# Attention with a sine and cosine mixture: sines in two pieces, other places for the splits of x and u, values copied at once

## The chip, the cores and the metric

The kernel runs on one core of one Trainium2 chip. The metric is device time in microseconds (us), median of several runs. The engines are TensorE (PE in the profile; its weight loads are PEld), VectorE (DVE), ScalarE (ACT), GpSimd (POOL) and SyncE (SP), which here only issues DMAs.

## What is computed

The reference, cut to what matters (8 batches, 8 heads, 576 positions, head size 64, model size 512):

```python
scores = (q @ k.T) / sqrt(64)
scores = where(scores >= max(scores) - tau, scores, -1e9)
attn = softmax(scores)
x = (attn @ v), heads side by side           # (8, 576, 512)
theta = x @ w_theta
zr, zi = x * cos(theta), x * sin(theta)
u = x + w_tok_r @ zr + w_tok_i @ zi          # over the positions
out = u + maximum(u @ w_ch, 0)
```

The attention part is float32. The four weight matrices come in as 8-byte floats, which the kernel converts on the chip. Products of the second half ("the mixture") are made from a high and a low part of each factor, in a faster 32-bit format (F32R), as three matmuls.

## The kernel before

**Attention.** Two heads make a pair; there are 32 pairs (numbered from 0), four to a batch, and nine half units to a pair: 288 steps of the loop in `tile_attn_moe`. A half unit is 128 query rows against all 576 keys. `score` has PE make the scores into one PSUM tile, DVE evict them with the row minimum (L302) and ACT take the exponential (L312). `mask` (L321) applies the threshold on DVE. `flip` and `flip_last` transpose the weights on PE (L365, L378), ACT copies them out (tile `a`, L370 to L385). `values` (L398) multiplies by v, 20 matmuls, twice per pair (first 256 rows, then 320), and ACT copies the result to `xT` (L399). `normalize` transposes the reciprocals of the row sums, and `scale` in it multiplies xT by them on DVE (L425, L428). Scores run three steps ahead of flips (AHEAD = 3). Inputs of the next pair are loaded and split at fixed steps of a pair: q at its steps 1 and 2 (ACT L242, L243, POOL L245), k at 4 and 5 (ACT L100, POOL L109).

**Mixture.** When a batch's four pairs are done, `start` splits its four x tiles in high and low parts (`split_x`: a cast on ACT or DVE, L100 or L104, then a subtraction on POOL or DVE, L109) and appends a generator `moe(b)`, which issues its work in small portions while the next batch's attention runs. The order of its parts is written out by hand (`ORDER`): `angle` ("a": product with w_theta, evicted by ACT L487 and DVE L488, reduced to turns on DVE L494, absolute value on ACT L497), `sines` ("s", for two chunks at a time: the sine table is loaded on ACT, L502, four sines taken, L507, each multiplied by x on POOL, L508, and the exponential's table loaded again, L510), `flip` in `moe` ("f": transposes on PE L524, high part by ACT L526, low part by DVE L513), `token` ("t": the product over positions, L542, added to x by DVE L545), then `split_u` for each chunk of u and the product with w_ch (L591 evicts it). The first product of each kind takes chunks 0 to 2 first and chunk 3 last.

**What sets the order.** All four engines run their instructions in the order in which the code issues them; attention's are moved a little ahead by priority. In each step the loop issues the next scores, exponential and mask, then `catch_up`, `fill`, the flips, `catch_up`, then the step's `todo` (values, normalize, start) behind a second `fill`. `fill` first advances one of two streams of weight loads (`streams`, in turn), then draws from the mixture until the PE time due (`share`) is spent; a generator that yields None ends the turn. `defer` puts a function off until a given number of `catch_up` calls. Values and normalize of a pair's end come one step after its last flip, start two steps after it (LAG = 3). PSUM has one double tile for scores and six tiles of one bank (`ps_t`) for all else, so a late copy out of PSUM keeps PE waiting. The eighth batch's mixture runs after the last pair, alone (`finish`).

**Weights.** `convert` turns 8-byte floats into 4-byte ones in many small DVE and ACT steps, the last on PE (w_ps, L164, L165). `split_weight` casts the high part on ACT (L171) and subtracts it for the low part on DVE (L174); `load_wtok` keeps both in SBUF for nine chunks (two halves each), `load_wm` sends them through DRAM.

Of the kernel before, what the change touches and what calls it, by code (L numbers as in the profile page):

```python
# [10 lines left out]
F32 = mybir.dt.float32  # L11
# [28 lines left out]
def tile_attn_moe(  # L40
# [33 lines left out]

    ident = const.tile([P, P], F32, name="ident")
    make_identity(nc, ident)

    small = const.tile([P, 4], F32, name="small")
    tau_sb = small[:, 0 : 1]
# [86 lines left out]
            got.append((slice(c, c + n2), ps))  # L166
        return got, flat

    def split_weight(got, hi, lo):
        for r, w in got:  # L170
            nc.scalar.copy(out=hi[:, r], in_=w)  # L171
        yield
        for r, w in got:
            nc.vector.tensor_tensor(out=lo[:, r], in0=w, in1=hi[:, r].bitcast(F32), op=ALU.subtract)  # L174

    def load_wtok(c):
        got, _ = yield from convert(w_tok[c * P : (c + 1) * P, :], S)
# [2 lines left out]
    def load_wm(which, src, c):  # L180
        got, flat = yield from convert(src[c * P : (c + 1) * P, :], DM, which == 0)
        hi, lo = flat[:, 0, :DM], flat[:, 1, :DM]
        yield from split_weight(got, hi, lo)
        for i, t in enumerate((hi, lo)):
            nc.sync.dma_start(
                wm_dram[which, :, :, i, c, :].rearrange("m p e -> p m e"),
                t.bitcast(F32).rearrange("p (m e) -> p m e", e=P),
            )
# [90 lines left out]
    def score(u, j):  # L279

        pr = u.pr
        ps = ps_s.tile([P, 2, 512], F32, tag="s", name="s_ps")
        if u.i < 4:
            c = u.i * P + (0 if j == 0 else SP + 64)
            parts = [(pr.qf[:, c : c + P], j, kk, 0) for kk in pr.keys[j]]
        else:
            parts = [(pr.qf[:, 512:SP], 0, kk, 0) for kk in pr.keys[0]]
            parts += [(pr.qf[:, S : S + P], 1, kk, 64) for kk in pr.keys[1]]
        for h in range(2):
            todo = []  # L290
            for st, jj, kk, turn in parts:
                k0 = (h * HS + turn) % S
                n1 = min(HS, S - k0)
                todo.append((st, 0, n1, kk[:, k0 : k0 + n1]))
                if n1 < HS:
                    todo.append((st, n1, HS, kk[:, 0 : HS - n1]))
            for x, (st, d0, d1, kk) in enumerate(todo):
                nc.tensor.matmul(ps[:, h, d0:d1], st, kk, start=(x == 0), stop=(x == len(todo) - 1))  # L298

        sc = pool.tile([P, S], F32, tag="sc", name="sc", bufs=2)  # L300
        u.ps.append(sc)
        nc.vector.tensor_scalar(  # L302
            out=sc.rearrange("p (a b) -> p a b", a=2),
            in0=ps[:, :, :HS],
            scalar1=-1.0,
            scalar2=None,
            op0=ALU.mult,
            op1=ALU.min,
            accum_out=u.nm[:, j : j + 1],
        )  # L310

        nc.scalar.activation(out=u.s[:, j], in_=sc, func=AF.Exp, bias=u.nm[:, j : j + 1], scale=-1.0)  # L312
        if j == u.m - 1:
            nc.vector.tensor_scalar(
                out=u.nm[:, 2 : 2 + u.m], in0=u.nm[:, : u.m], scalar1=span, scalar2=None, op0=ALU.add
            )

    def mask(u, j):
# [11 lines left out]
        if u.i == 4:  # L330
            defer(lambda: nc.scalar.copy(out=u.sf[:, S:SP], in_=u.sf[:, 512:S]))
            invert(u.pr)

    waiting = []

    def defer(fn, n=1):
        waiting.append([n, fn])

    def catch_up(everything=False):
        now = []  # L340
        for w in list(waiting):
            w[0] -= 1
            if w[0] <= 0 or everything:
                waiting.remove(w)
                now.append(w[1])
        for fn in now:
            fn()
# [39 lines left out]
    def values(pr, g):  # L387

        t = pr.a[g]
        w = t.w  # L390
        if pr.n not in xT:
            xT[pr.n] = pool.tile([P, S], F32, tag="xT", name=f"xT{pr.n}", bufs=8)
        o = ps_t.tile([P, 512], F32, tag="t", name="o_ps")
        for c in range(5):
            for j in range(2):
                st = pr.v[:, 4 * j + c, :] if c < 4 else pr.v5[:, j, :]
                mv = t.a[:, c, j, :] if c < 4 else t.a5
                nc.tensor.matmul(o[64 * j : 64 * j + 64, :w], st, mv, start=(c == 0), stop=(c == 4))  # L398
        defer(lambda: nc.scalar.copy(out=xT[pr.n][:, 256 * g : 256 * g + w], in_=o[:, :w]))  # L399

    def invert(pr):
        rows = pr.rows
# [11 lines left out]
    def normalize(pr):  # L414
# [12 lines left out]
                r = slice(64 * j, 64 * j + 64)  # L427
                nc.vector.tensor_tensor(out=x[r, 512:S], in0=x[r, 512:S], in1=tl[r, 64 * j : 64 * j + 64], op=ALU.mult)  # L428

        defer(scale, 2)  # L430

    def product(wm, parts, todo, together):

# [30 lines left out]
    def split_x(b):  # L464
        parts[b] = []
        for c in range(NM):
            hi, lo = halves("x")
            split(nc.vector if c == NM - 1 else nc.scalar, nc.vector if c == NM - 1 else nc.gpsimd, hi, lo, xT[b * NP + c])
            parts[b].append((hi, lo))

    def moe(b):
        last = b == B - 1
# [7 lines left out]
        def angle(m):  # L480
# [13 lines left out]
            nc.vector.scalar_tensor_tensor(  # L494
                out=th, in0=km, scalar=MAGIC, in1=th, op0=ALU.subtract, op1=ALU.subtract
            )
            defer(lambda: nc.scalar.activation(out=km, in_=th, func=AF.Abs))  # L497
            zs[m, "f"] = z

        def sines(ms):  # L500

            nc.scalar.preload_act_table(AF.Sin)  # L502
            for m in ms:
                z = zs.pop((m, "f"))
                x = xT[b * NP + m]
                for zi, scale, bias in ((z[:, :S], -TURN_IN, half_pi), (z[:, S:], -TURN_IN, 0.0)):
                    nc.scalar.activation(out=zi, in_=zi, func=AF.Sin, scale=scale, bias=bias)  # L507
                    lo_eng.tensor_tensor(out=zi, in0=zi, in1=x, op=ALU.mult)  # L508
                zs[m] = z
            nc.scalar.preload_act_table(AF.Exp)  # L510

        def low(zl, tv, zh):
            defer(lambda: nc.vector.tensor_tensor(out=zl, in0=tv, in1=zh.bitcast(F32), op=ALU.subtract))  # L513

        def flip(m):
            z = zs.pop(m)
# [13 lines left out]
            zs[m, "T"] = out  # L530

        def token(m):
            catch_up(True)
            zz = zs.pop((m, "T"))
            x = xT[b * NP + m]
            for h in range(2):
# [4 lines left out]
                for n, (z, w) in enumerate(work):  # L541
                    nc.tensor.matmul(ps[:, :HS], z, w, start=(n == 0), stop=(n == len(work) - 1))  # L542
                    if n % 3 == 2:
                        yield 393
                nc.vector.tensor_tensor(out=x[:, hs], in0=ps[:, :HS], in1=x[:, hs], op=ALU.add)  # L545

        us = {}

        def split_u(c):
            hi, lo = halves("u")  # L550
            split(nc.vector, nc.vector if c == NM - 1 else nc.gpsimd, hi, lo, xT[b * NP + c])
            us[c] = (hi, lo)

        done = []
# [1 line left out]
        for what in ORDER.split():  # L556
# [10 lines left out]
                    yield cost  # L567
                left -= 1
            elif what == "s":
                defer(lambda ms=ms: sines(ms), 2)  # L570
                yield None
            elif what == "f":
                yield from flip(m)
            else:
# [4 lines left out]
                        yield next(other, 0)  # L579
                for cost in other:  # L580
                    yield cost
                done.append(m)
            while left == 0 and done:
                split_u(done.pop(0))
        yield None
# [20 lines left out]
    def fill():  # L606

        with at(-5, 0):
            next(streams[step[0] % 2], None)
            step[0] += 1  # L610
            if step[0] > 2 * (per + 8):
                next(late, None)
# [39 lines left out]
    with tc.manual_schedule(engines={nc.tensor.engine, nc.vector.engine, nc.scalar.engine, nc.gpsimd.engine}):  # L652
# [11 lines left out]
        for t, (n, i, j) in enumerate(halfs):  # L664
# [8 lines left out]
            with tc.high_priority(offset=ATTENTION):  # L673
                u = units[n, i]
                flip(u, j)
                if j == 1 or i == 4:
                    flip_last(u)
                    del units[n, i]
            catch_up()
            if (i, j) == (1, 1):  # L680
                todo.setdefault(t + 1, []).append((values, (pr, 0)))
            if i == 4:
                todo.setdefault(t + 1, []).extend([(values, (pr, 1)), (normalize, (pr,))])
                if n % NP == NP - 1:
                    todo.setdefault(t + LAG - 1, []).append((start, (n // NP,)))
            fill()
            with tc.high_priority(offset=ATTENTION):
                if n + 1 < B * NP:
# [17 lines left out]
        for t in sorted(todo):  # L706
            for fn, a in todo[t]:
                fn(*a)
            catch_up()
            catch_up()  # L710
        finish()


# [44 lines left out]
```

## Time and profile before

| | |
|---|---|
| median of 3 runs | 1275.32 us (1273.94 to 1278.27) |
| the profiled execution's own time | 1274.94 us |
| its span, first to last instruction | 1273.1 us |
| mean granted TensorE clock | 0.944 |
| busy: PE, DVE, ACT, POOL | 1104.8, 846.8, 756.2, 345.2 us |

An engine's busy share says little alone, as the stages differ: some 129 us of attention with weight conversion, seven stretches of about 148 to 162 us in which attention of one batch and the mixture of the batch before share PE, and a last one of some 85 us with a mixture alone. In waits, "A <- B" reads: A stood idle until B's instruction released it. The clock is the share of full speed that PE was granted (1.0 is 2.4 GHz, 0.5 is 1.2 GHz).

### The profile page before, as it was taken

The numbers are of one execution on the slowest core, as the hardware profiler recorded it, in microseconds if no ns is written. First come the engines' busy times: TensorE is split into PE (matmuls) and PEld (weight loads), VectorE is DVE, ScalarE is ACT, GpSimd is POOL, SyncE is SP. The second block draws the span as 40 slices with busy tenths as digits, with TensorE's granted clock in tenths as the row PEclk, the third lists the DMA queues.
The fourth block names the chain that finished last, engine by engine and source line by source line (L and its number), as shares of the span: only waits on it lengthen the run. The fifth ranks groups of instructions, "written<-read, shape, count | busy, mean of one in ns | idle before, by whom it ended". The sixth has DMA issues, their size and how long they took to land.

```text
span 1273.1 us, 20988 instructions
## 1 busy us (share of the span) xinstructions
PE 1104.8 (87%) x7736; PEld 961.2 (75%) x7736; DVE 846.8 (67%) x1979; ACT 756.2 (59%) x1444; POOL 345.2 (27%) x239
## 2 busy tenths in 40 slices
PE   5868786898789988899879997899888998799988
PEld 4546575787778877788768876788778887688888
DVE  6878777877557765677656765577656766567553
ACT  5656567655676556765576547765567655765350
POOL 1111143121532222421332215322224212332100
PEclk9878898999989998999989999999899999899989
DMA  6542222234211143113321142111431133210311
GB/s 216 151 120 80 62 73 75 81 114 150 79 54 47 55 125 98 44 48 97 108 78 48 48 150 79 49 50 58 125 102 40 47 89 103 91 47 1 112 59 55
DMA packets 55174, 105.24 MB, mean 83 GB/s; under 512 B 11936, under 2 KB 20128, under 8 KB 55072
## 3 DMA queue, kind: packets, MB, share of 16 engines
q1 hardware_dynamic: 55072, 103.91, 27.0%
q8 instruction: 61, 1.00, 0.3%
q14 instruction: 41, 0.34, 0.1%
HBM read 90.24 MB, written 13.63 MB: 82 GB/s over the span
## 4 chain that ended last, share of the span: by engine, by line
PE 63%; ACT 16%; DVE 13%; issue 4%; POOL 2%; DMA 0%; SPq 0%; ACTq 0%; DVEq 0%; POOLq 0%
PE y_ps L542 13%; PE o_ps L398 13%; PE m_ps L448 12%; PE s_ps L298 12%; PE t_ps L365 6%; DVE sc L302 4%; DVE s_sb L321 3%; ACT s_sb L312 2%; PE z_ps L524 2%; ACT z L507 2%; ACT L510 2%; ACT L502 2%; ACT a L370 1%; PE rb_ps L417 1%; POOL xl L109 1%
## 5 line engine op out<-in xcount | busy, mean ns | idle before, releaser
L312 ACT ACTIVATE s_sb<-sc,nm 128x576 f32<-128x576 f32 x288 | 223.7, 777 | 397.1 <-DVE sc L302 396.8
L302 DVE TENSOR_SCALAR_CACHE_REDUCE sc<-s_ps 128x576 f32<-128x576 f32 x288 | 216.8, 753 | 224.8 <-PE s_ps L298 223.1
L298 PE MATMUL s_ps<-k,qq 128*128 128x288 f32 (+1 forms) x1344 | 252.7, 315 | 57.8 <-DVE sc L302 40.7
L321 DVE SCALAR_TENSOR_TENSOR s_sb<-sc,nm,s_sb 128x576 f32<-128x576 f32 x288 | 282.0, 979 | 13.5 <-ACT s_sb L312 4.2
L298 PEld LDWEIGHTS s_ps<-k,qq 128*128 128x128 f32 x1344 | 200.3, 198 | 91.2 <-DVE sc L302 43.4
L245 POOL TENSOR_TENSOR qq<-qraw,qq 64x576 fp32r<-64x576 f32 x62 | 95.3, 1541 | 387.3 <-ACT qq L243 201.4
L542 PE MATMUL y_ps<-wt_h,zh 128*128 128x288 f32 x576 | 170.1, 313 | 24.6 <-DVE zl L513 13.1
L365 PE MATMUL t_ps<-ident,s_sb 128*128 128x128 f32 x1152 | 183.9, 285 | 0.3 <-DVE wt_l L174 0.3
L398 PE MATMUL o_ps<-a,v 128*64 128x320 f32 (+1 forms) x1280 | 172.3, 414 | 0.9 <-ACT a L370 0.9
L542 PE MATMUL y_ps<-wt_l,zh 128*128 128x288 f32 x576 | 166.3, 306 | 0.0
L109 POOL TENSOR_TENSOR k<-kraw,k 128x576 fp32r<-128x576 f32 x62 | 96.0, 1549 | 250.9 <-ACT k L100 229.7
L370 ACT COPY a<-t_ps 128x512 f32<-128x512 f32 x256 | 148.2, 579 | 24.9 <-PE t_ps L365 24.0
L365 PEld LDWEIGHTS t_ps<-ident,s_sb 128*128 128x128 f32 x1152 | 149.9, 147 | 3.2 <-issue 1.1
L398 PEld LDWEIGHTS o_ps<-a,v 128*64 128x64 f32 x1280 | 87.4, 138 | 64.3 <-issue 10.1
L542 PEld LDWEIGHTS y_ps<-wt_h,zh 128*128 128x128 f32 x576 | 111.5, 194 | 29.1 <-DVE zl L513 15.7
L448 PE MATMUL m_ps<-xh,wm 128*128 128x288 f32 x512 | 109.4, 345 | 23.6 <-ACT xh L100 23.6
L508 POOL TENSOR_TENSOR z<-z,xT 128x576 f32<-128x576 f32 x56 | 80.2, 1462 | 136.8 <-ACT z L507 136.8
L542 PEld LDWEIGHTS y_ps<-wt_l,zh 128*128 128x128 f32 x576 | 111.9, 194 | 0.0
L448 PEld LDWEIGHTS m_ps<-xh,wm 128*128 128x128 f32 x512 | 87.4, 222 | 29.3 <-ACT xh L100 29.0
L542 PE MATMUL y_ps<-wt_h,zl 128*128 128x288 f32 x576 | 102.7, 304 | 0.0
L448 PE MATMUL m_ps<-uh,wm 128*128 128x288 f32 x512 | 88.6, 310 | 0.8
L524 PE MATMUL z_ps<-ident,z 128*128 128x128 f32 x288 | 54.0, 302 | 34.9 <-ACT a L370 28.7
(81 smaller groups left out, 1534.2 us busy)
## 6 DMA issues: line engine op xcount, KB each, us to landing
wm<-wm_dram SPq DMA_DIRECT2D x64, 512.0 KB, 3.6
qraw<-in_qT_dram SPq DMA_DIRECT2D x128, 144.0 KB, 3.4
kraw<-in_kT_dram SPq DMA_DIRECT2D x128, 144.0 KB, 2.9
out_dram<-xT SPq DMA_DIRECT2D x32, 288.0 KB, 4.0
v<-in_vp_dram SPq DMA_DIRECT2D x32, 256.0 KB, 2.7
wraw<-in_w_tok_dram SPq DMA_DIRECT2D x9, 576.0 KB, 4.8
wm_dram<-wraw SPq DMA_DIRECT2D x16, 256.0 KB, 2.3
wraw<-in_w_theta_dram SPq DMA_DIRECT2D x4, 512.0 KB, 5.8
```

The lines of the kernel that those rows point to most:

```text
L109: eng_lo.tensor_tensor(out=lo, in0=src, in1=hi.bitcast(F32), op=ALU.subtract)
L245: eng.tensor_tensor(out=qq[64:128], in0=raw[64:128], in1=qq[64:128].bitcast(F32), op=ALU.subtract)
L298: nc.tensor.matmul(ps[:, h, d0:d1], st, kk, start=(x == 0), stop=(x == len(todo) - 1))
L302: nc.vector.tensor_scalar(out=sc.rearrange("p (a b) -> p a b", a=2), in0=ps[:, :, :HS], scalar1=-1.0, scalar2=None, op0=ALU.mult, op1=ALU.min,
L312: nc.scalar.activation(out=u.s[:, j], in_=sc, func=AF.Exp, bias=u.nm[:, j : j + 1], scale=-1.0)
L321: nc.vector.scalar_tensor_tensor(out=e, in0=u.ps[j], scalar=u.nm[:, 2 + j : 3 + j], in1=e, op0=ALU.is_le, op1=ALU.mult, accum_out=u.pr.row ...
L365: nc.tensor.transpose(out=tp[:, c * P : (c + 1) * P], in_=u.sf[:, k0 + c * P : k0 + (c + 1) * P], identity=ident)
L370: nc.scalar.copy(out=t.a[:, :, j, q0 : q0 + P], in_=tp.rearrange("p (c q) -> p c q", c=4))
L398: nc.tensor.matmul(o[64 * j : 64 * j + 64, :w], st, mv, start=(c == 0), stop=(c == 4))
L448: nc.tensor.matmul(tiles[h][:, :HS], wm[:, a, c, :], parts[c][bb][:, hs], start=(count[h] == 0), stop=(count[h] == 11))
L508: lo_eng.tensor_tensor(out=zi, in0=zi, in1=x, op=ALU.mult)
L542: nc.tensor.matmul(ps[:, :HS], z, w, start=(n == 0), stop=(n == len(work) - 1))
```

## The change

- A constant `minus` (the identity times -1) is made; the low parts of the token weights are made by a PE matmul that subtracts the high part in PSUM and an ACT copy, in place of a DVE subtraction.
- `split_x`: the casts of chunks 0 and 1 stay on ACT, chunk 2's goes to DVE (low part on POOL), chunk 3 (DVE, DVE) is deferred by one `catch_up`.
- `start` is issued one step earlier, in the step of the last values; `scale` is deferred by one `catch_up` in place of two; the copy of the values' result is issued at once.
- `sines` becomes a generator: one chunk a step. The first piece loads the sine table, the last loads the exponential's. An exponential that comes up between is held and issued behind the last piece. The absolute values that are still deferred are issued before a series; `token` flushes only the deferred low parts.
- Chunk 3 of u is split in halves on DVE inside `token`, behind each half's addition.
- `fill` advances only one of the two weight streams in the first seven turns (steps with an even count).
- In the tail, both sine pieces are issued on the spot.

```diff
--- before.py
+++ after.py
@@ -74,6 +74,8 @@
 
     ident = const.tile([P, P], F32, name="ident")
     make_identity(nc, ident)
+    minus = const.tile([P, P], F32R, name="minus")
+    nc.vector.tensor_scalar(out=minus, in0=ident, scalar1=-1.0, scalar2=None, op0=ALU.mult)
 
     small = const.tile([P, 4], F32, name="small")
     tau_sb = small[:, 0 : 1]
@@ -166,12 +168,16 @@
             got.append((slice(c, c + n2), ps))
         return got, flat
 
-    def split_weight(got, hi, lo):
+    def split_weight(got, hi, lo, on_pe=True):
         for r, w in got:
             nc.scalar.copy(out=hi[:, r], in_=w)
         yield
         for r, w in got:
-            nc.vector.tensor_tensor(out=lo[:, r], in0=w, in1=hi[:, r].bitcast(F32), op=ALU.subtract)
+            if on_pe:
+                nc.tensor.matmul(w, minus, hi[:, r], start=False, stop=True, skip_group_check=True)
+                nc.scalar.copy(out=lo[:, r], in_=w)
+            else:
+                nc.vector.tensor_tensor(out=lo[:, r], in0=w, in1=hi[:, r].bitcast(F32), op=ALU.subtract)
 
     def load_wtok(c):
         got, _ = yield from convert(w_tok[c * P : (c + 1) * P, :], S)
@@ -180,7 +186,7 @@
     def load_wm(which, src, c):
         got, flat = yield from convert(src[c * P : (c + 1) * P, :], DM, which == 0)
         hi, lo = flat[:, 0, :DM], flat[:, 1, :DM]
-        yield from split_weight(got, hi, lo)
+        yield from split_weight(got, hi, lo, False)
         for i, t in enumerate((hi, lo)):
             nc.sync.dma_start(
                 wm_dram[which, :, :, i, c, :].rearrange("m p e -> p m e"),
@@ -309,7 +315,13 @@
             accum_out=u.nm[:, j : j + 1],
         )
 
-        nc.scalar.activation(out=u.s[:, j], in_=sc, func=AF.Exp, bias=u.nm[:, j : j + 1], scale=-1.0)
+        def exponential():
+            nc.scalar.activation(out=u.s[:, j], in_=sc, func=AF.Exp, bias=u.nm[:, j : j + 1], scale=-1.0)
+
+        if held[0]:
+            held.append(exponential)
+        else:
+            exponential()
         if j == u.m - 1:
             nc.vector.tensor_scalar(
                 out=u.nm[:, 2 : 2 + u.m], in0=u.nm[:, : u.m], scalar1=span, scalar2=None, op0=ALU.add
@@ -331,16 +343,36 @@
             defer(lambda: nc.scalar.copy(out=u.sf[:, S:SP], in_=u.sf[:, 512:S]))
             invert(u.pr)
 
+    held = [False]
+    series = []
+
+    def sine_piece():
+
+        if not series:
+            return
+        if not held[0]:
+            nc.scalar.preload_act_table(AF.Sin)
+            held[0] = True
+        if next(series[0], None) is None:
+            series.pop(0)
+            if not series:
+                nc.scalar.preload_act_table(AF.Exp)
+                now = held[1:]
+                held[:] = [False]
+                for fn in now:
+                    fn()
+
     waiting = []
 
-    def defer(fn, n=1):
-        waiting.append([n, fn])
-
-    def catch_up(everything=False):
+    def defer(fn, n=1, kind=None):
+        waiting.append([n, fn, kind])
+
+    def catch_up(only=None):
         now = []
         for w in list(waiting):
-            w[0] -= 1
-            if w[0] <= 0 or everything:
+            if only is None:
+                w[0] -= 1
+            if w[0] <= 0 or only is not None and w[2] == only:
                 waiting.remove(w)
                 now.append(w[1])
         for fn in now:
@@ -396,7 +428,7 @@
                 st = pr.v[:, 4 * j + c, :] if c < 4 else pr.v5[:, j, :]
                 mv = t.a[:, c, j, :] if c < 4 else t.a5
                 nc.tensor.matmul(o[64 * j : 64 * j + 64, :w], st, mv, start=(c == 0), stop=(c == 4))
-        defer(lambda: nc.scalar.copy(out=xT[pr.n][:, 256 * g : 256 * g + w], in_=o[:, :w]))
+        nc.scalar.copy(out=xT[pr.n][:, 256 * g : 256 * g + w], in_=o[:, :w])
 
     def invert(pr):
         rows = pr.rows
@@ -427,7 +459,7 @@
                 r = slice(64 * j, 64 * j + 64)
                 nc.vector.tensor_tensor(out=x[r, 512:S], in0=x[r, 512:S], in1=tl[r, 64 * j : 64 * j + 64], op=ALU.mult)
 
-        defer(scale, 2)
+        defer(scale)
 
     def product(wm, parts, todo, together):
 
@@ -465,8 +497,13 @@
         parts[b] = []
         for c in range(NM):
             hi, lo = halves("x")
-            split(nc.vector if c == NM - 1 else nc.scalar, nc.vector if c == NM - 1 else nc.gpsimd, hi, lo, xT[b * NP + c])
             parts[b].append((hi, lo))
+            if c < 2:
+                split(nc.scalar, nc.gpsimd, hi, lo, xT[b * NP + c])
+            elif c == 2:
+                split(nc.vector, nc.gpsimd, hi, lo, xT[b * NP + c])
+            else:
+                defer(lambda: split(nc.vector, nc.vector, hi, lo, xT[b * NP + c]), 1)
 
     def moe(b):
         last = b == B - 1
@@ -494,23 +531,22 @@
             nc.vector.scalar_tensor_tensor(
                 out=th, in0=km, scalar=MAGIC, in1=th, op0=ALU.subtract, op1=ALU.subtract
             )
-            defer(lambda: nc.scalar.activation(out=km, in_=th, func=AF.Abs))
+            defer(lambda: nc.scalar.activation(out=km, in_=th, func=AF.Abs), 1, "abs")
             zs[m, "f"] = z
 
         def sines(ms):
 
-            nc.scalar.preload_act_table(AF.Sin)
-            for m in ms:
+            for k, m in enumerate(ms):
                 z = zs.pop((m, "f"))
                 x = xT[b * NP + m]
                 for zi, scale, bias in ((z[:, :S], -TURN_IN, half_pi), (z[:, S:], -TURN_IN, 0.0)):
                     nc.scalar.activation(out=zi, in_=zi, func=AF.Sin, scale=scale, bias=bias)
                     lo_eng.tensor_tensor(out=zi, in0=zi, in1=x, op=ALU.mult)
                 zs[m] = z
-            nc.scalar.preload_act_table(AF.Exp)
+                yield None if k == len(ms) - 1 else True
 
         def low(zl, tv, zh):
-            defer(lambda: nc.vector.tensor_tensor(out=zl, in0=tv, in1=zh.bitcast(F32), op=ALU.subtract))
+            defer(lambda: nc.vector.tensor_tensor(out=zl, in0=tv, in1=zh.bitcast(F32), op=ALU.subtract), 1, "low")
 
         def flip(m):
             z = zs.pop(m)
@@ -530,7 +566,7 @@
             zs[m, "T"] = out
 
         def token(m):
-            catch_up(True)
+            catch_up(only="low")
             zz = zs.pop((m, "T"))
             x = xT[b * NP + m]
             for h in range(2):
@@ -543,12 +579,17 @@
                     if n % 3 == 2:
                         yield 393
                 nc.vector.tensor_tensor(out=x[:, hs], in0=ps[:, :HS], in1=x[:, hs], op=ALU.add)
+                if m == NM - 1:
+                    if h == 0:
+                        us[m] = halves("u")
+                    hi, lo = us[m]
+                    split(nc.vector, nc.vector, hi[:, hs], lo[:, hs], x[:, hs])
 
         us = {}
 
         def split_u(c):
             hi, lo = halves("u")
-            split(nc.vector, nc.vector if c == NM - 1 else nc.gpsimd, hi, lo, xT[b * NP + c])
+            split(nc.vector, nc.gpsimd, hi, lo, xT[b * NP + c])
             us[c] = (hi, lo)
 
         done = []
@@ -567,8 +608,13 @@
                     yield cost
                 left -= 1
             elif what == "s":
-                defer(lambda ms=ms: sines(ms), 2)
-                yield None
+                catch_up(only="abs")
+                series.append(sines(ms))
+                if step[0] is None:
+                    while series:
+                        sine_piece()
+                else:
+                    yield None
             elif what == "f":
                 yield from flip(m)
             else:
@@ -579,7 +625,8 @@
                         yield next(other, 0)
                 for cost in other:
                     yield cost
-                done.append(m)
+                if m < NM - 1:
+                    done.append(m)
             while left == 0 and done:
                 split_u(done.pop(0))
         yield None
@@ -606,7 +653,8 @@
     def fill():
 
         with at(-5, 0):
-            next(streams[step[0] % 2], None)
+            if step[0] % 2 == 0 or step[0] > 6:
+                next(streams[step[0] % 2], None)
             step[0] += 1
             if step[0] > 2 * (per + 8):
                 next(late, None)
@@ -677,12 +725,13 @@
                     flip_last(u)
                     del units[n, i]
             catch_up()
+            sine_piece()
             if (i, j) == (1, 1):
                 todo.setdefault(t + 1, []).append((values, (pr, 0)))
             if i == 4:
                 todo.setdefault(t + 1, []).extend([(values, (pr, 1)), (normalize, (pr,))])
                 if n % NP == NP - 1:
-                    todo.setdefault(t + LAG - 1, []).append((start, (n // NP,)))
+                    todo.setdefault(t + 1, []).append((start, (n // NP,)))
             fill()
             with tc.high_priority(offset=ATTENTION):
                 if n + 1 < B * NP:
@@ -707,7 +756,8 @@
             for fn, a in todo[t]:
                 fn(*a)
             catch_up()
-            catch_up()
+        catch_up()
+        step[0] = None
         finish()
```

## Rows read from the trace of the kernel before

**Rows 1.** Page, part 1: busy time, share of the span, instructions.

```profile
PE 1104.8 (87%) x7736; PEld 961.2 (75%) x7736; DVE 846.8 (67%) x1979; ACT 756.2 (59%) x1444; POOL 345.2 (27%) x239
```

**Rows 2.** Windows: pair 13, pair 14, batch 3; us, PE, PEld, DVE, ACT, POOL busy, PEclk.

```profile
488.30:531.30 43.00, 34.10 (x236) 29.73 (x235) 23.27 (x60) 32.71 (x59) 17.41 (x12) 0.92 0.25 76
531.30:563.60 32.30, 31.45 (x244) 28.03 (x244) 23.74 (x58) 19.57 (x40) 8.95 (x6) 1.00 0.17 47
...
450.40:598.20 147.80, 131.19 (x958) 115.69 (x958) 96.96 (x232) 91.72 (x176) 45.24 (x30) 0.97 0.26 77
```

**Rows 3.** Waits of PE, batch 3 (450.4 to 598.2 us): total, times, longest.

```profile
PE z_ps L524 <- ACT a L370: 4.1, 1, 4.1
PE m_ps L448 <- ACT xh L100: 3.3, 3, 3.0
PE y_ps L542 <- DVE zl L513: 1.8, 1, 1.8
PE y_ps L542 <- ACT xT L399: 1.4, 1, 1.4
PE m_ps L448 <- DVE ul L109: 1.3, 1, 1.3
PE z_ps L524 <- DVE zl L513: 1.2, 1, 1.2
PE t_ps L378 <- ACT xT L399: 0.8, 1, 0.8
PE m_ps L448 <- POOL xl L109: 0.8, 1, 0.8
```

**Rows 4.** Timeline of ACT, 458 to 471 us: start, us, instruction, idle before.

```profile
465.30 0.78 ACT L312 ACTIVATE s_sb<-sc,nm 128x576 f32<-128x576 f32 x1 [4.78 <-DVE sc L302]
...
468.33 1.81 ACT L100 CAST xh<-xT 128x576 fp32r<-128x576 f32 x3
```

**Rows 5.** Timeline of PE, 459 to 464 us.

```profile
460.27 2.91 PE L398 MATMUL o_ps<-a,v 128*64 128x320 f32 x20
```

**Rows 6.** Timeline of DVE, 459 to 590 us.

```profile
464.44 0.76 DVE L302 TENSOR_SCALAR_CACHE_REDUCE sc<-s_ps 128x576 f32<-128x576 f32 x1 [3.61 <-PE s_ps L298]
...
585.96 1.84 DVE L109 TENSOR_TENSOR ul<-xT,uh 128x576 fp32r<-128x576 f32 x1
```

**Rows 7.** Timeline of ACT, 486 to 525 us.

```profile
489.08 0.78 ACT L312 ACTIVATE s_sb<-sc,nm 128x576 f32<-128x576 f32 x1 [1.44 <-DVE sc L302]
...
491.37 1.28 ACT L502 ACT_TABLE_LOAD   x1
...
496.56 0.62 ACT L408 COPY rb<-rows 128x512 f32<-128x512 f32 x1
...
510.15 0.78 ACT L312 ACTIVATE s_sb<-sc,nm 128x576 f32<-128x576 f32 x1 [4.46 <-DVE sc L302]
```

**Rows 8.** Windows: from the first sines, and behind them (columns as before).

```profile
491.37:505.69 14.32, 10.18 (x60) 9.60 (x60) 7.51 (x19) 12.70 (x23) 5.48 (x4) 0.76 0.17 55
498.00:504.50 6.50, 5.73 (x26) 5.73 (x27) 5.23 (x13) 4.93 (x13) 1.00 (x1) 0.50 0.01 3
```

**Rows 9.** Groups by line: busy us, mean ns, idle before.

```profile
L502 ACT ACT_TABLE_LOAD x16 | 20.5, 1283 | 0.3
...
L174 DVE TENSOR_TENSOR wt_l<-w_ps,wt_h 128x288 fp32r<-128x288 f32 x18 | 6.9, 442 | 0.0
L171 ACT CAST wt_h<-w_ps 128x288 fp32r<-128x288 f32 x18 | 6.9, 398 | 4.1 <-PE w_ps L165 4.1
```

**Rows 10.** Windows: the first batch of pairs (columns as before).

```profile
10.40:139.20 128.80, 99.72 (x541) 72.02 (x541) 106.35 (x248) 79.74 (x155) 23.72 (x16) 0.89 0.43 132
```

**Rows 11.** Waits of PE, 10.4 to 139.2 us.

```profile
PE s_ps L298 <- DVE sc L302: 24.2, 21, 3.4
```

**Rows 12.** Waits of PE, 1187 us to the end.

```profile
PE m_ps L448 <- POOL xl L109: 1.7, 2, 1.5
PE y_ps L542 <- ACT zh L526: 1.5, 1, 1.5
```

## The prediction

> **What bounds the kernel now.** I read the page's shares first, then windows, then PE's waits, then the timelines of the engines that PE waited for. TensorE (PE) is busy 87% of the span and every other engine under 70% [rows 1], so the question is where PE stands idle. The windows answer it by stage: batch 3, from the scores of its boundary to those of the next (147.8 us), holds 131.2 us of PE work, so 16.6 us idle, while its dearest pair (13 of 32, 43.0 us) alone holds 8.9 of them, with ACT busy 32.7 of 43.0 there and the clock at 0.92 [rows 2]. The waits name the places: eight waits, 14.7 us together, once each per batch (the xh one in three pieces) [rows 3]; the batches from 3 to 6 repeat them almost to the hundredth. Each belongs to something the change touches. A second loss hangs on them: for 6.5 us behind the longest wait PE ran at clock 0.50, its lower level of 1.2 GHz, although it was busy 5.7 of these [rows 8]. The mean clock of 0.97 over the batch [rows 2] means some 0.03 x 2 x 147.8 = 9 us at half speed, which cost at most half of that, 4.4 us. The first 129 us are another regime: no mixture runs yet, VectorE (DVE) is busy 106.4 of 128.8 us [rows 10], and PE waits 24.2 us for DVE's score evictions [rows 11].
>
> **The change part by part, per batch.** PE's work per batch stays the same, so a batch gets shorter by what PE idles less.
>
> *Splits of x, and the start one step earlier.* At the boundary ACT is idle 4.78 us until 465.30, then does the exponential and a queue of older work, and the three xh casts run only from 468.33, 1.81 us for three [rows 4]; the first product waits 3.3 us in all [rows 3]. After the change the start is issued right behind the values product and the copy of its result. That product ends at 460.27 + 2.91 = 463.18 [rows 5]. The copy (320 columns, so under the 0.60 us of a 576-column cast) and two casts end near 463.18 + 0.5 + 1.2 = 464.9, all inside ACT's idle time. The third cast goes to DVE, which is idle 3.61 us until 464.44 [rows 6], so it costs nothing; without that cover it would be some 0.5 us before the next score eviction. The fourth split is deferred by one turn because its scaling is; the first product takes chunk 3 last, so 18 matmuls cover it. PE reaches the first product after the score and flips of that step, about 465. I take 2.7 of 3.3 us (bounds 0 and 3.3). The POOL wait for xl (0.8) I leave: the low parts start earlier, but so does PE's want of them (bounds -0.8 and 0.8).
>
> *Last u in halves.* DVE took 1.84 us for the low part [rows 6], and PE waited 1.3 [rows 3]. Now half 0 is split while PE does half 1 of the token product, and half 1 leaves half the work. Two more DVE instructions per batch fall on an engine busy 97.0 of 147.8 us [rows 2]. I take 1.2 (0 to 1.3).
>
> *Values copied at once.* The copy stood behind the next exponential, and a PSUM buffer with it: PE waited 1.4 and 0.8 us [rows 3]. Moved ahead, it waits for its own 20 matmuls at the head of ACT's queue; behind it stands the next exponential, whose scores come after those matmuls on PE anyway. I take 1.3 (0 to 2.2), as another ACT copy will be the next late one.
>
> *Sines in two pieces.* Two sets of two table loads and four sines block ACT: from 491.37 to 496.56, 5.2 us [rows 7]. A piece is half, 2.6 us, and the second is followed by the held exponential, 0.8. Everything of the mixture is now a step earlier, so the first set's first piece falls where ACT idles 1.44 us before 489.08, and the second set's first piece where it idles 4.46 us before 510.15 [rows 7]. But from 491.37 to 505.69 ACT worked 12.70 of 14.32 us [rows 8]: its work there can't shrink, only slide. So of the 4.1 us of the first set I take 1.5 (0 to 4.1), of 1.8 + 1.2 at the second 1.8 (0 to 3.0). What is late next: the flips' copies behind the second piece. The mask of a held exponential comes a step later on DVE, and its flip two steps after that, so I cost the hold at nothing; without this room it would be one piece, 2.6 us, per set.
>
> Between the pieces ACT now runs copies and Abs with the sine table loaded, which no row shows. Bounds: nothing, or two more loads of 1.283 us [rows 9] per set, 16 x 2 x 1.283 = 41 us of ACT time in all. I take nothing, being nearest to the kernel before, where loads stand only at its preload lines. The Trainium skill (ScalarE: Activation LUTs, Table sets: the hidden batching unit) says that cheap functions such as copy and abs are in every table set; by that it is nothing too.
>
> *Clock.* With shorter waits I take 1.9 of the 4.4 us back (0 to 4.4).
>
> *Sum.* 2.7 + 1.2 + 1.3 + 1.5 + 1.8 + 1.9 = 10.4 us a batch. Seven of the eight batches run beside attention: 73 us.
>
> *Token weights' low parts.* Eighteen subtractions of 0.442 us leave DVE, 8.0 us; eighteen copies like the casts of 0.398 us join ACT, 7.2 us [rows 9], and 18 matmuls join PE, each well under 0.3 us (20 of 320 columns took 2.91 [rows 5]). They lie in the DVE-bound beginning, where ACT is busy 79.7 of 128.8 us [rows 10]. DVE is not always the last, and each new copy waits for PE: 3 us of gain (-4 to 8). Half the early turns of the second weight stream are left out; its work comes three steps later, long before a product needs it: 0 (-2 to 2). The constant's one instruction lies before the first score: 0.
>
> *Tail.* The eighth batch runs alone; PE waits there, among others, 1.7 us for xl and 1.5 for zh [rows 12]. Sines at once instead of two turns later: 1.5 us (-2 to 4).
>
> Together 73 + 3 + 1.5 = 77.5 us off the profiled execution's 1274.9 us, 0.4 under the median of 1275.3: **1198 us**.
>
> **The rivals.**
> 1. *ACT stays the bound in the sine stretch*: the pieces only move its work. For it: 12.70 of 14.32 us [rows 8]. Against: the idle 4.46 us just behind [rows 7]. Then only the boundary, u, one buffer wait and some clock are won: 2.7 + 1.2 + 0.8 + 0.9 = 5.6 a batch, 39 us, and 3 at the start: 1233 us.
> 2. *Table reloads between the pieces*: the 41 us of ACT above, nearly all on the path, against a gain of 77: about 1239 us.
> 3. *The gaps come back elsewhere*: PE runs on into the next late copy, or into DVE's evictions, and nothing is won but a few us: 1272 us. For it: ACT and DVE are at two thirds over the batch [rows 2]; against: where such waits are rare PE is nearly full, 31.5 of 32.3 us in pair 14 [rows 2].
> 4. *Slower: the values copy at the head of ACT's queue.* It waits up to 2.91 us [rows 5] at 64 places. If flips' copies or evictions that are ready stand behind it, PE starves. It decides from 77.5 / 64 = 1.2 us of lost PE time at each; at 1.5 us it gives 1274.9 - 77.5 + 96 = 1293 us. Against: ACT has nothing to do there now, idle 4.78 and 4.46 us [rows 4, 7].
>
> **How the numbers follow.** Forecast 0.56, ACT stays the bound 0.22, reloads 0.03, gaps come back 0.10, slower 0.09. The range leaves out the last two: its upper end, 1250, lies above rivals 1 and 2; its lower end, 1165, is a batch gaining 15 us (the boundary 3, u and values 3, most of the sines' 7, half the clock). A measurement of this kernel tells 0.3% (4 us) from no change. Faster by more: 0.56 + 0.22 + 0.03 and half of rival 3 make 0.86; within: 0.05; slower: 0.09.
>
> **What would show it.** In PE's waits of a middle batch: the one for xh under 0.6 us, that for ul gone, those for the values copy gone, the one for the a copy near 2.6, those for zl near 1.2 together; ACT's timeline with the table load, two sines, copies, two sines, the load, an exponential. A batch then takes some 137 us instead of 148. The first 129 us lose about 3. More than two table loads a set would mean rival 2. An ACT idle before the values copies, with PE waiting for older copies, would mean rival 4; windows behind the sines with ACT full and PE waiting as long as before, rival 1. A batch at 146 us or more makes the forecast wrong.

## The result and the profile after

1215.45 us (1215.15 to 1215.98, 4 runs) against 1276.14 before (four runs now): ratio 0.9525, 95% interval 0.9507 to 0.9543. The profiled execution's span went from 1273.1 to 1214.1 us. Windows of the changed kernel (columns as in [rows 2]): batch 3, pair 13, the first batch of pairs.

```profile
431.60:571.50 139.90, 128.77 (x958) 114.54 (x958) 97.89 (x236) 92.07 (x175) 45.00 (x30) 0.98 0.27 82
465.70:506.10 40.40, 33.86 (x247) 29.93 (x247) 24.93 (x60) 32.15 (x59) 17.25 (x13) 0.96 0.27 78
11.00:134.70 123.70, 99.84 (x550) 74.15 (x551) 104.38 (x235) 82.69 (x164) 22.89 (x15) 0.92 0.44 134
```

Batch 3 is 7.9 us shorter [rows 2]: 5.5 from less idle PE (16.6 to 11.1), 2.4 from less busy time for the same 958 matmuls, with the granted clock at 0.98 instead of 0.97. The seven batches lost 54.8 us, 7.8 on average; the beginning 5.1 [rows 10]; the tail, in which the last batch's mixture runs alone, nothing (85.7 before, 86.0 after). PE's waits in batch 3 after, against [rows 3]:

```profile
PE s_ps L304 <- POOL k L111: 4.7, 3, 3.2
PE t_ps L410 <- ACT xT L431: 1.8, 1, 1.8
PE m_ps L480 <- POOL xl L111: 1.6, 2, 1.2
PE z_ps L560 <- DVE zl L549: 0.9, 1, 0.9
PE s_ps L304 <- ACT k L102: 0.7, 1, 0.7
PE z_ps L560 <- ACT a L402: 0.5, 1, 0.5
PE m_ps L480 <- ACT a L402: 0.5, 1, 0.5
PE y_ps L578 <- DVE zl L549: 0.4, 1, 0.4
PE m_ps L480 <- ACT xh L102: 0.2, 1, 0.2
```

The waits for xh, ul, zl and the flip's copy are gone or small, as forecast; of the two for the values copy (xT) one is left, with 1.8 us. The longest is new: the next pair's keys. Timelines of the changed kernel at the first sine set, ACT first:

```profile
465.11 1.28 ACT L354 ACT_TABLE_LOAD   x1
466.40 0.78 ACT L543 ACTIVATE z<-z,small 128x576 f32<-128x576 f32 x1
467.09 0.67 ACT L543 ACTIVATE z<-z 128x576 f32<-128x576 f32 x1
467.66 0.66 ACT L102 CAST k<-kraw 128x576 fp32r<-128x576 f32 x1
...
471.02 1.28 ACT L359 ACT_TABLE_LOAD   x1
472.32 0.78 ACT L319 ACTIVATE s_sb<-sc,nm 128x576 f32<-128x576 f32 x1
```

then POOL:

```profile
467.26 2.80 POOL L544 TENSOR_TENSOR z<-z,xT 128x576 f32<-128x576 f32 x2 [2.29 <-ACT z L543]
470.02 1.91 POOL L111 TENSOR_TENSOR k<-kraw,k 128x576 fp32r<-128x576 f32 x1
```

The second key's cast stands behind the first piece, and its low part on POOL behind that piece's two products; the scores got it at 471.98. Before, batch 3 had but this wait for the keys:

```profile
PE s_ps L298 <- POOL k L109: 0.7, 1, 0.7
```

### The profile page after: what moved, and what is told of

Its sections match the earlier page's. It is cut to its first block, busy times and chain, and to the rows that moved or that the text cites. A ratio compares the mean times of both kernels' runs of the same rounds, so it can differ in the third digit from the quotient of the medians.

```text
span 1214.1 us, 21049 instructions
## 1 busy us (share of the span) xinstructions
PE 1085.7 (89%) x7754; PEld 951.9 (78%) x7754; DVE 853.3 (70%) x1986; ACT 764.8 (63%) x1454; POOL 345.1 (28%) x239
## 4 chain that ended last, share of the span: by engine, by line
PE 59%; DVE 16%; ACT 14%; issue 5%; POOL 4%; DMA 1%; SPq 1%; POOLq 0%; ACTq 0%; DVEq 0%
PE y_ps L578 13%; PE m_ps L480 13%; PE s_ps L304 11%; PE o_ps L430 10%; PE t_ps L397 7%; DVE sc L308 4%; DVE s_sb L333 4%; ACT s_sb L319 3%; POOL k L111 2%; ACT z L543 2%; ACT a L402 2%; PE z_ps L560 2%; ACT L354 2%; DVE z L531 1%; POOL z L544 1%
## 5 line engine op out<-in xcount | busy, mean ns | idle before, releaser
L304 PE MATMUL s_ps<-k,qq 128*128 128x288 f32 (+1 forms) x1344 | 249.1, 312 | 74.9 <-POOL k L111 36.1
L333 DVE SCALAR_TENSOR_TENSOR s_sb<-sc,nm,s_sb 128x576 f32<-128x576 f32 x288 | 277.8, 964 | 18.3 <-ACT s_sb L319 6.9
L402 ACT COPY a<-t_ps 128x512 f32<-128x512 f32 x256 | 147.3, 575 | 10.4 <-PE t_ps L397 9.9
L480 PE MATMUL m_ps<-xh,wm 128*128 128x288 f32 x512 | 97.6, 319 | 1.8 <-ACT xh L102 1.8
L111 POOL TENSOR_TENSOR ul<-xT,uh 128x576 fp32r<-128x576 f32 x24 | 34.4, 1431 | 196.5 <-ACT zh L562 96.5
L480 PE MATMUL m_ps<-uh,wm 128*128 128x288 f32 x512 | 85.8, 301 | 3.2 <-ACT a L402 3.2
L578 PEld LDWEIGHTS y_ps<-wt_h,zl 128*128 128x128 f32 x576 | 85.3, 193 | 0.0
```

The costliest lines, as they stand in the source:

```text
L111: eng_lo.tensor_tensor(out=lo, in0=src, in1=hi.bitcast(F32), op=ALU.subtract)
L333: nc.vector.scalar_tensor_tensor(out=e, in0=u.ps[j], scalar=u.nm[:, 2 + j : 3 + j], in1=e, op0=ALU.is_le, op1=ALU.mult, accum_out=u.pr.row ...
L402: nc.scalar.copy(out=t.a[:, :, j, q0 : q0 + P], in_=tp.rearrange("p (c q) -> p c q", c=4))
L480: nc.tensor.matmul(tiles[h][:, :HS], wm[:, a, c, :], parts[c][bb][:, hs], start=(count[h] == 0), stop=(count[h] == 11))
```

## The experiments

Each kernel is the changed one with the edit shown, cut to its main lines ("..." marks a cut). Ratios are to the kernel before, measured beside each run, with their 95% interval; the changed kernel has 0.9525.

**Sines whole, at the earlier place.**

```diff
-        if next(series[0], None) is None:
-            series.pop(0)
+        while series:
+            if next(series[0], None) is None:
+                series.pop(0)
+        if held[0]:
...
```

> The changed kernel with both sine pieces of a set issued in one turn, all else as changed. The changed kernel took 1215 us; a middle batch now has a PE wait of 3.2 us for the keys' low part on POOL, behind the first set. Theory A (that wait comes from the earlier start, which puts the first set onto the steps where the next pair's keys are cast and split, and the pieces only soften it): ACT is held 5.2 us at once, the second key's cast comes 2.6 us later and four products stand before its low part on POOL, so this wait grows to 5 to 6 us and the kernel takes 1235 to 1250 us. Theory B (the wait comes from cutting the sines in two, which stretches them over two steps): it falls below 2 us and the kernel takes 1215 us or less.

1256.8 us, 0.9863 (0.9845 to 0.9881). Its waits:

```profile
PE s_ps L304 <- POOL k L111: 4.7, 3, 3.3
PE t_ps L412 <- ACT xT L433: 4.4, 1, 4.4
PE s_ps L304 <- ACT k L102: 3.3, 1, 3.3
```

The keys' waits go from 5.4 to 8.0 us, as theory A had it, and xT from 1.8 to 4.4, which it had not: both by the 2.6 us of a piece. The time lies 7 us beyond A's range. The pieces are worth 41 us here, and theory B falls.

**Start, scaling and splits of x as before.**

```diff
-  todo.setdefault(t + 1, []).append((start, (n // NP,)))
+  todo.setdefault(t + LAG - 1, []).append((start, (n // NP,)))
...
-        defer(scale)
+        defer(scale, 2)
...
```

(and the old body of `split_x`, and the second `catch_up` in the last loop)

> The changed kernel with the start, the scaling and the splits of x where they were before (start two steps after the last flip, scaling two turns later, three casts on ACT); the sines stay in pieces. Theory A: the keys' waits (4.7 us a batch) fall under 1 us, as the first set lies behind the key casts again, while the wait for xh comes back with 3 us and the one for a flip's copy with 1 to 3 us; 1215 to 1230 us. Theory B: the keys' wait stays at 3 us and the xh wait comes on top, 1240 us or more. Theory C (ACT is full in this stretch, and a wait removed at one place returns at another): as A in the keys, with the sum of PE's waits in a batch unchanged to 1 us.

1257.6 us, 0.9868 (0.9847 to 0.9888).

```profile
PE z_ps L555 <- DVE zl L544: 4.4, 2, 3.9
PE m_ps L480 <- ACT xh L102: 3.0, 3, 2.7
PE t_ps L397 <- ACT a L404: 2.6, 1, 2.6
PE s_ps L304 <- DVE sc L308: 2.2, 3, 1.5
```

It is 42 us slower than the changed kernel. The keys' waits fall to 1.6 us (under 1 was expected), xh and the flip's copy come back as expected, but zl with 4.4 and the score evictions with 2.2 were in no theory. The time lies in B's range, but the keys' wait fell, which B denied; and PE idles 15.3 us in batch 3 instead of 11.1, so C falls too. Before the long zl wait DVE stood at a mask, for an exponential held behind the second piece, and then for ACT's cast of zh, which came later still:

```profile
513.29 1.55 DVE L333 SCALAR_TENSOR_TENSOR s_sb<-sc,nm,s_sb 128x576 f32<-128x576 f32 x1 [3.84 <-ACT s_sb L319]
...
515.49 0.29 DVE L544 TENSOR_TENSOR zl<-z_ps,zh 128x128 fp32r<-128x128 f32 x1 [0.64 <-ACT zh L557]
```

The place of the start decides what the pieces collide with: here zl, in the changed kernel the keys. With either the pieces or the earlier start undone, only some 17 of the 60 us are left; they pay together.

**Values copy deferred again.**

```diff
-        nc.scalar.copy(out=xT[pr.n][...], in_=o[:, :w])
+        defer(lambda: nc.scalar.copy(out=xT[pr.n][...], in_=o[:, :w]))
```

> The changed kernel with the copy of the values' result deferred by one turn again. Theory A: the copy falls behind the next exponential, and at the second sine set perhaps behind its second piece; the waits for xT grow from 1.8 us a batch to 3 or 4 us, 10 to 20 us in all, 1225 to 1235 us. Rival (the copy at the head of ACT's queue costs as much as it frees): 1210 to 1218 us.

1203.6 us, 0.9447 (0.9428 to 0.9466): faster by 12 (10 by the ratios), which neither view had. ACT's timeline in the tail of the changed kernel, then of this one:

```profile
1139.57 0.42 ACT L431 COPY xT<-o_ps 128x320 f32<-128x320 f32 x1 [2.69 <-PE o_ps L430]
1139.90 1.25 ACT L102 CAST xh<-xT 128x576 fp32r<-128x576 f32 x2
```

```profile
1129.93 1.25 ACT L102 CAST xh<-xT 128x576 fp32r<-128x576 f32 x2
1132.60 0.43 ACT L431 COPY xT<-o_ps 128x320 f32<-128x320 f32 x1 [1.42 <-PE o_ps L430]
```

The xh casts need only older tiles. Behind the copy they wait for 20 matmuls, and POOL's three low parts (4.9 us) after them. Half the gain lies in the tail, 86.0 to 79.6 us; 4.7 us of that is PE's busy time for the same 536 matmuls (76.05 to 71.36).

**Splits of chunks 0 to 2 ahead of the values product.** `split_x` takes a list of chunks:

```diff
+    def early(b):
+        finish()
+        split_x(b, (0, 1, 2))
...
+                if n % NP == NP - 1:
+                    todo.setdefault(t + 1, []).append((early, (n // NP,)))
                 todo.setdefault(t + 1, []).extend([(values, (pr, 1)), (normalize, (pr,))])
```

> The changed kernel with the splits of x chunks 0 to 2 issued ahead of the last values product and its copy, in the same step; the copies stay at once. The deferred copy gained 12 us; theory D: not because the copy is better late, but because at the boundary it stands at the head of ACT's queue for 20 matmuls in front of two xh casts that are ready, and POOL's low parts follow those. Then this kernel keeps that gain: the wait for xl falls from 1.6 us a batch to under 0.6, that for xh to 0, the tail takes 80 us in place of 86, and the wait for xT stays at 1.8 us where the deferred copy had 3.7; 1195 to 1204 us. Theory E (the copy is better late everywhere, also in mid pair): the gain doesn't come, 1210 to 1217 us.

1191.9 us, 0.9356 (0.9341 to 0.9371), 24 us better than the changed kernel (22 by the ratios). In batch 3:

```profile
PE t_ps L410 <- ACT xT L431: 1.8, 1, 1.8
...
PE m_ps L480 <- POOL xl L111: 0.7, 1, 0.7
```

The xh wait is gone, xT stays, the tail takes 80.1 us: theory D, though xl stays just above the 0.6 expected and the time came out 3 us under D's range. Batch 3 loses only 0.6 us of idle time by it and 2.1 of busy time, and the mean granted clock over the span goes from 0.959 to 0.974. One thing more came with the earlier splits: DVE's low part of chunk 3 takes 0.76 us, where it took 1.85 in the changed kernel:

```profile
L111 DVE TENSOR_TENSOR xl<-xT,xh 128x576 fp32r<-128x576 f32 x8 | 14.8, 1846 | 0.3
```

What share of the gain that has was not measured.

**Low parts of the keys on DVE** (pair 1 of a batch).

```diff
-        split(nc.scalar, nc.gpsimd if n else nc.vector, k1, k2, raw)
+        split(nc.scalar, nc.vector if n == 0 or n % NP == 1 and n > NP else nc.gpsimd, k1, k2, raw)
```

> The changed kernel with the keys' low parts of the second pair of each batch (the pair prepared while the first sine set runs) on DVE in place of POOL. Theory A: PE's wait for them falls from 3.2 us to under 1 us (cast on ACT, then 0.8 us of DVE), a batch gets 2.5 to 3.5 us shorter, seven batches and some clock: 1190 to 1198 us. Theory C (ACT is full there, the wait returns at another place): the keys' wait falls but the waits for flips' copies or zl grow by as much, 1208 to 1216 us.

1223.1 us, 0.9596 (0.9575 to 0.9617): slower by 8 than the changed kernel, outside both ranges. The longest wait of PE in batch 3, and DVE's timeline:

```profile
PE s_ps L304 <- DVE sc L308: 4.4, 2, 3.9
```

```profile
472.89 0.93 DVE L111 TENSOR_TENSOR k<-kraw,k 128x576 fp32r<-128x576 f32 x1 [3.45 <-ACT k L102]
473.74 0.75 DVE L308 TENSOR_SCALAR_CACHE_REDUCE sc<-s_ps 128x576 f32<-128x576 f32 x1
```

DVE waits for ACT's late cast with the next scores behind it. The wait moved to DVE's queue, at the head of which it was put; that ACT is full (theory C) isn't needed for it, and the next run bears that out.

**Second key cast and split on DVE alone**, on top of the splits first:

```diff
+        own = j == 1 and n % NP == 1 and n > NP
+        split(nc.vector if own else nc.scalar, nc.vector if own or n == 0 else nc.gpsimd, k1, k2, raw)
```

> The splits of x first (1192 us), and the second key of the pair prepared during the first sine set is cast and split on DVE alone, so that it waits neither for ACT (cast behind a sine piece) nor for POOL (low part behind the sines' products). The kernel with only the low parts on DVE failed because DVE stood waiting for ACT's cast for 3.5 us with the next scores behind it; here DVE needs only the loaded key, and 1.3 us of work. Theory A: the keys' waits fall from 5.7 us a batch to under 2, a batch gets 3 to 4 us shorter and the kernel takes 1160 to 1172 us. Theory C (ACT is full, the wait moves to flips' copies): 1183 to 1192 us.

1176.9 us, 0.9223 (0.9204 to 0.9243), the best of all, 15 us under the kernel with the splits first. Its batch 3:

```profile
PE t_ps L398 <- ACT a L403: 2.2, 1, 2.2
PE s_ps L305 <- POOL k L111: 1.7, 2, 1.2
```

The keys' waits fall from 5.7 to 1.7 us as expected; 2.2 us return at a flip's copy. The time lies between the ranges of A (up to 1172) and C (from 1183): most of A holds, with a part of C.

**Sines a step later.**

```diff
-                series.append(sines(ms))
...
+                    defer(lambda ms=ms: series.append(sines(ms)), 4)
```

> The changed kernel with each set of sines one step later, still in pieces. Theory A (the keys' wait is a collision of the first set with the key casts and low parts at steps 4 and 5 of the pair): the keys' waits fall from 5.4 us a batch to under 2 us and the second set falls behind the values copy, so the xT wait of 1.8 us goes; flips of the mixture may wait for POOL's products, 1 to 3 us; 1185 to 1205 us. Theory C (ACT is full, the wait only moves): waits for flips' copies or products grow by as much, 1212 to 1225 us.

1204.8 us, 0.9454 (0.9437 to 0.9472), at A's upper end. The keys' waits fall only to 3.4 us (under 2 was expected), xT goes, and the mixture's flips wait 3.3 us for POOL's products.

**Pieces at the end of the step**, behind values copies and key casts, on top of the splits first (`sine_piece()` moved behind the `todo` loop).

> The splits of x first (1192 us), and each sine piece issued at the end of its step, behind the values copies and key casts of that step, in place of ahead of them. At the second set the values copy then stands before the piece: the wait for xT, 1.8 us a batch, goes. At the first set the order on POOL is the same, half a step earlier: the keys' wait of 3.2 us changes by 1 us either way. Theory A: 1172 to 1185 us. Theory C (ACT is full in this stretch, waits only move): 1188 to 1195 us.

1206.4 us, 0.9454 (0.9437 to 0.947), 14 slower than without and outside both ranges, though the wait for xT went as expected. With the second key on DVE as well:

> Both: splits of x first, sine pieces at the end of the step, second key on DVE. Theory A: the two gains add, 1145 to 1165 us. Theory C: no better than the better of the two alone within 4 us.

1207.2 us, 0.9462 (0.9445 to 0.948): the gains don't add, and it is 30 us slower than with the second key alone, which neither theory had. In the first of the two PE and DVE wait so (DVE from 479 to 494 us), and the second shows both waits with the same lengths:

```profile
PE z_ps L560 <- DVE zl L549: 4.1, 1, 4.1
```

```profile
DVE s_sb L333 <- ACT s_sb L319: 4.4, 1, 4.4
```

```profile
487.76 1.44 ACT L319 ACTIVATE s_sb<-sc,nm 128x576 f32<-128x576 f32 x2
```

The piece now ends so late that two exponentials are held (the row of ACT above); DVE waits for the first at a mask, with the low part zl behind it. Both theories missed that.

**u whole, weights on DVE, both streams at once** (each part of the change undone by itself: `split_u` takes chunk 3 again, `load_wtok` passes False to `split_weight`, and for the streams the edit below).

```diff
-  if step[0] % 2 == 0 or step[0] > 6:
-      next(streams[step[0] % 2], None)
+  next(streams[step[0] % 2], None)
```

> The changed kernel with chunk 3 of u split whole, behind the token product, as before. By the sum behind the forecast: a wait for ul of 1.3 us comes back in each batch, 7 x 1.2 = 8 us and up to 6 us of clock: 1222 to 1230 us. Rival (the start one step earlier has moved POOL's work away from this split, so it is short anyway): 1214 to 1218 us.

> The changed kernel with the token weights' low parts made by DVE again. The first 129 us got 5.2 us shorter with the change, and batch 1, in which the last of these chunks fall, 4.2. By the sum behind the forecast they are worth 3 us (-4 to 8): 1218 us. Rival (all of the beginning's gain is theirs): 1221 to 1226 us. Rival (the streams' first turns make it): 1214 to 1217 us.

> The changed kernel with both weight streams running from the first turn, as before. The first 129 us got 5.2 us shorter with the change, and neither the place of the weights' subtraction nor the values copy made more than 1 us of that. If the streams' order makes it, this takes 1218 to 1222 us; if, as the sum behind the forecast had it, it is worth 0 (-2 to 2), 1213 to 1217 us.

u whole: 1213.3 us, 0.9525 (0.951 to 0.954), no difference, and no wait for ul. The split is short without the halves:

```profile
L111 DVE TENSOR_TENSOR ul<-xT,uh 128x576 fp32r<-128x576 f32 x8 | 6.1, 760 | 0.3
```

It took 1.84 us in [rows 6]; with the late start even the halves took 871 ns each, against 459 in the changed kernel. Weights on DVE: 1217.5 us, 0.9555 (0.9532 to 0.9579); the intervals overlap, so 2 us, if any, and in its trace they lie in batch 1 (159.5 us instead of 157.6), not in the first batch of pairs (124.0 instead of 123.7). Both streams: 1221.5 us, 0.9572 (0.9555 to 0.9589), and the first batch of pairs takes 131.1 us instead of 123.7:

```profile
10.30:141.40 131.10, 100.52 (x553) 72.11 (x553) 103.32 (x237) 83.50 (x167) 24.27 (x16) 0.92 0.42 130
```

The beginning's gain is the streams'.

## Why the forecast was right, and where not

Faster, inside the range, 18 us short of 1198. Of the signs that the forecast named, those for xh, ul, zl and the sines' timeline came; the wait for the values copy stayed, and a batch takes 139.9 us, not 137. That the time lies so near is in part luck: terms that were too small and terms that were too large made up for each other. Term by term:

- **Splits of x (2.7 a batch).** 3.3 of xh became 0.2, but xl went from 0.8 to 1.6. The forecast laid copy and casts one behind the other and found ACT's idle time long enough; it left the order of the two unquestioned, and POOL's low parts, which begin only after them, at zero (bounds -0.8 and 0.8, and the xl wait grew by 0.8). Turning the order gave 24 us.
- **Values copied at once (1.3).** The waits were 2.2 and are 1.8. Rival 4 named this queue and spoke of lost PE time at 64 places; what decides is the one place in a batch where casts stand behind the copy. There the order cost 24 us; deferring every copy gave back 12. The sentence that only the next exponential stands behind it was the failing step.
- **Sines (1.5 + 1.8).** The three waits fell from 7.1 to 1.8 us, more than forecast; but the sets moved a step earlier, past the keys' casts on ACT and low parts on POOL, and 4.7 us of new wait took most of it. The step "what is late next" looked at ACT's copies alone. Rival 1 falls: with two queues cleared (splits first, second key on DVE), nearly the same ACT work (91.2 us, here 92.1) goes into batches of 135 us. Rival 3 holds in part: the eight waits of [rows 3] fell from 14.7 to 5.4 us, and 4.7 came back at the keys.
- **The hold (0).** Right where the change has it; with the pieces half a step later it cost a wait of 4.4 us, with the late start one of 3.8.
- **u (1.2).** The wait went, but by luck: with u whole again it stays away. With the earlier start the split begins before POOL's next subtraction and no longer behind its start (the last section has the rows).
- **Clock (1.9).** About 2.4 in batch 3, taken as the fall of PE's busy time.
- **Beginning (3) and tail (1.5).** 5.1 and -0.3. The first comes near by luck: the weights' 3 are near zero there, and the streams, costed at 0, make it. In the tail the waits for zh, an eviction and a sine's product are unchanged, and the one for xl grew from 1.7 to 2.1.
- **Seven times the middle batch.** Batches 1 and 7 gained 4.2 and 5.5 us, not the 8 to 10 of the others.

No reload came between the pieces (rival 2): the changed kernel loads tables as often as before,

```profile
L354 ACT ACT_TABLE_LOAD x16 | 20.5, 1283 | 0.2
L359 ACT ACT_TABLE_LOAD x16 | 20.5, 1283 | 0.3
```

with copies and casts running between the sines. No Abs falls between them here; with the sines a step later one does in each batch, and its loads are 16 and 16 too:

```profile
470.91 0.67 ACT L534 ACTIVATE z<-z 128x576 f32<-128x576 f32 x1
```

These traces agree with what the Trainium skill (ScalarE: Activation LUTs, Table sets: the hidden batching unit) says of such functions.

## What to carry to other kernels

When work moves to another step, list for each in-order queue what is ready and stands behind it there: here two casts behind a copy cost 24 us, and one key behind a sine piece 15. Cutting a blocking stretch in pieces can pay (41 us), and where the pieces stand matters as much: half a step later they cost 14 us. Undo parts one by one: one part of this change cost time, one did nothing, and one costed at zero gave 6 us.

## What was not expected of the hardware

A DVE subtraction of two SBUF tiles of 128x576 (the low part ul) took 0.76 us with POOL idle and 1.84 us where POOL's subtraction had begun before it, at 585.48 us, beside the 585.96 of [rows 6]:

```profile
585.48 1.70 POOL L245 TENSOR_TENSOR qq<-qraw,qq 64x576 fp32r<-64x576 f32 x1 [1.04 <-ACT qq L243]
```

With u whole it begins before POOL's, and now POOL's takes longer (1.75 us, where others take 1.43):

```profile
555.89 0.76 DVE L111 TENSOR_TENSOR ul<-xT,uh 128x576 fp32r<-128x576 f32 x1
```

```profile
556.19 1.75 POOL L251 TENSOR_TENSOR qq<-qraw,qq 64x576 fp32r<-64x576 f32 x1 [13.23 <-PE s_ps L304]
```

The Trainium skill (SBUF — State Buffer, Who interferes with whom) says that a DVE instruction with two SBUF inputs contends with a GpSimd instruction that reads SBUF, and that the order of issue decides which of them is held up; these rows agree with that. In the changed kernel the same slowness moved to x's chunk 3 (1.85 us, shown with the splits first).

Removing short waits gave more than their length. Between the changed kernel and the one with the splits first, PE's idle time over the span fell by 5.3 us, its busy time for the same matmuls by 19.3 (the changed kernel first):

```profile
PE 1085.7 (89%) x7754; PEld 951.9 (78%) x7754; DVE 853.3 (70%) x1986; ACT 764.8 (63%) x1454; POOL 345.1 (28%) x239
```

```profile
PE 1066.4 (90%) x7754; PEld 936.1 (79%) x7754; DVE 840.1 (71%) x1986; ACT 763.9 (64%) x1454; POOL 339.8 (29%) x239
```

The mean granted clock was 0.959 and 0.974 of full speed. With levels of 1.2 and 2.4 GHz that is some 100 and 62 us at the lower one; 38 us less at half speed make 19 us less busy time, so the clock can account for it. Which waits make it fall stayed open: in the kernel before, the waits for ul, 1.35 us each, were followed by half speed in some batches (736.8 to 740.2 us) and not in others (587.9 to 591.3 us).
